# LayerNorm sums from VectorE to ScalarE, wider exponentials and another order of the last products, in an attention and MLP kernel

## The chip, the cores and the metric

The kernel runs on one core of a Trainium2 chip. The metric is the device time of one execution in microseconds (us). In what follows PE is TensorE (matmuls; PEld its weight loads), DVE is VectorE, ACT is ScalarE, POOL is GpSimd and SP is SyncE, which here only issues DMAs.

## The reference

There are 8 batch entries, 8 heads, 576 rows and 64 columns per head. First an attention without a score matrix:

```python
q_s = exp(q - max(q, -1));  q_s /= sum(q_s, -1)          # over the 64 columns
k_s = exp(k - max(k, 2));   k_s /= sum(k_s, 2)           # over the 576 rows
kv  = einsum('bhsd,bhse->bhde', k_s, v)
x   = einsum('bhsd,bhde->bhse', q_s, kv)                  # -> (8, 576, 512)
```

Then, on each row of x (512 columns), a LayerNorm with a gain and a two-layer MLP with a residual:

```python
xn  = (x - mean(x)) / sqrt(var(x) + 1e-6) * g_ln
out = x + relu(xn @ w_ch1) @ w_ch2                        # w_ch1 512x2048, w_ch2 2048x512
```

## The kernel before, in words

**Stages.** The rows are handled as nine chunks c of 512 rows (`T` = 4 tiles of 128). Chunks 0 to 7 are the first 512 rows of the batch entries; chunk 8 (`C9`) collects the 64 rows that each of the eight entries has over. Every chunk goes through the MLP once: a stage. A stage's matmuls are written as a list of steps by `mlp_steps`, and `run` merges a list of side jobs into it: a side job is a pair of a step number and a function, and its instructions are put into every engine's program just ahead of that step. The order is by hand (`tc.manual_schedule`): each engine executes its own instructions in the order in which the program writes them. So "step 34" in what follows is a place in this order, not a time.

**One stage.** For c of 2 (`FAST`) and more, steps 0 to 64 are the first layer, `mm1` (L347): 16 groups of four matmuls of 512 columns into a PSUM tile `ph`, each followed by a relu on ACT (L335) into `hT`. There are six PSUM buffers for these and the second layer's tiles (`mm_ps`), and two for the attention (`att_ps`). Steps 64 to 120 are the second layer, `mm2_fast`: seven products of 16 matmuls of 256 columns each (`prod`, L454; half a step per matmul), in place of eight, after a scheme of Strassen's kind. It needs sums of blocks of `hT` (`sum_h`, L438, DVE), sums of the weights (made once), and sums of the products: ACT copies the accumulating bank `a` at three points (`seed_c` at L548, and `copy_u` at L493 for `s2` and `s3`), and DVE adds these copies to bank `b` (`add_u`, L496; `seed_e` puts one sum into bank `e`). `y_quarter` (L468, DVE) makes a quarter of an output tile: the bank times `rstd` plus `x`. When both halves of a tile are there, POOL stores it.

**Beside it.** In stage c stand, as side jobs, the attention of chunk c + 1 (`attn_fast`) and the preparation of entry c + 2 (`load_batch`, `prep_fast`):

- `load_batch` at step 1 loads q, k, v over SP; a write by DVE into each buffer ahead of it (L818) makes the load wait until the buffer's last reader is done. `qt` has two buffers, `kt` and `vt` one.
- `prep_fast` puts on ACT the exponentials of q (`exp_q`, L175) and of k (`exp_k`, L142), two heads or 512 columns at a time, casts of v (`cast_v`, L150), and the left-over rows of k and v (`prep_kvrem`). `eq_T` transposes the exponentials by a DMA from SP.
- `attn_fast` has the 20 `kv_mm` matmuls, then 4 `po_mm` for each tile t. `x_out` on DVE takes `po` from PSUM: the product with the reciprocal sums (L314), then `stats`: `bn_stats` (L300), `bn_aggr` (L301), and `xn` = (x - mean) * gain (L302). `xn_T` at steps 60 and 101 transposes `xn` by DMA from SP, two tiles at a time; the next stage's `mm1` reads both. `rstd_op` on ACT gives 1/sqrt(var + eps) as an exponential of a logarithm (L328, L329).
- In stage 7 the attention is that of chunk 8, with `attn_side`: 16 `po_mm` of 256 columns at even distances from step 14 to 92, products in four parts per tile (L292), and the same `stats`.

**The last stage** (chunk 8) has no side jobs but `sum_h`. Its products are ordered by `last_products`: the product 4 goes last, into a bank of its own (`d`), with `pre` adding the rest of that quarter beforehand. Tiles 2 and 3 are stored by halves of 256 columns (`store_rest`), 64 rows over SP and 64 over ACT, tiles 0 and 1 whole over POOL.

Of the kernel before, what the change touches and what calls it, by code (L numbers as in the profile page):

```python
# [14 lines left out]
AF = mybir.ActivationFunctionType  # L15
ALU = mybir.AluOpType
# [4 lines left out]
def kernel(  # L21
# [21 lines left out]
    P = 128  # L43
# [90 lines left out]

    eks, eqs, eqTs, xs, xnTs, rstds = {}, {}, {}, {}, {}, {}

    def exp_k(b, j):
        kt = raws[b][0]
        if j == 0:
            eks[b] = att.tile([P, T, H, D], BF16, tag="ek", name="ek")  # L140
        hs = slice(2 * j, 2 * j + 2)
        nc.scalar.activation(  # L142
            eks[b][:, :, hs, :].rearrange("p t h d -> p h t d"), kt[:, hs], AF.Exp
        )
# [23 lines left out]
        )  # L168
        eqTs[c] = att.tile([P, T, NP, P], BF16, tag="eqT", name="eqT")

    def exp_q(b, j):
        if j == 0:
            new_eq(b)
        hs = slice(2 * j, 2 * j + 2)
        nc.scalar.activation(  # L175
            eqs[b][0][:, :, hs, :].rearrange("p t h d -> p h t d"),
            raws[b][2][:, hs], AF.Exp,
        )
# [119 lines left out]
    def stats(c, t, src):  # L298
# [5 lines left out]
            op0=ALU.subtract, op1=ALU.mult,  # L304
        )

    def x_out(c, t):

        x = xs[c][0]
        if c == 1 or (c == 0 and t < 2):  # L310
            stats(c, t, pobox[c, t])
            return
        if c < B:
            nc.vector.tensor_mul(  # L314
                x[:, t].rearrange("p (h d) -> p h d", h=H),
                pobox[c, t].rearrange("p (h d) -> p h d", h=H),
                eqs[c][2][:, t].to_broadcast([P, H, D]),
            )
        stats(c, t, x[:, t])
# [4 lines left out]
    def rstd_op(c):  # L324
        mv = xs[c][3]
        lnv = sml.tile([P, T], FP32, tag="lnv", name="lnv")
        rstds[c] = mlp.tile([P, T], FP32, tag="rstd", name="rstd")
        nc.scalar.activation(lnv, mv[:, :, 1], AF.Ln, bias=eps_ln)  # L328
        nc.scalar.activation(rstds[c], lnv, AF.Exp, scale=-0.5)  # L329

    def relu(i, dst, src, fast):
# [105 lines left out]
        )[i]  # L437
        nc.vector.tensor_tensor(out=dst, in0=x, in1=y, op=op)  # L438

    def prod(n, bank, t, k, first=False, last=False, own=False):  # L440

        at = slice(t * P, t * P + P)
        if n in (1, 2, 4):
            odd, half = ((0, 0), (1, 0), None, (1, 1))[n - 1]
            lhsT = hbox["h"][:, 2 * k + odd, 2 * half + t, :]
        else:
            lhsT = hbox["s"][:, {5: 0, 6: 1, 7: 2, 3: 3}[n], k, at]
        if n in (1, 2):
            rhs = w2_sb[:, 2 * k + n - 1, 0:DH2]
        elif n == 3:  # L450
            rhs = w2_sb[:, 2 * k + 1, DH2:DM]
        else:
            rhs = w2_q[:, {5: 0, 6: 1, 7: 2, 4: 3}[n], k]
        nc.tensor.matmul(hbox[bank][:, t], lhsT, rhs, start=first and (own or t == 0) and k == 0,  # L454
                         stop=k == KH - 1, skip_group_check=True)

    def bank(name):
        hbox[name] = mm_ps.tile([P, 2, DH2], FP32, tag="m", name="b" + name)

    def new_y(c, t):  # L460
        if (c, t) not in ybox:
            ybox[c, t] = outp.tile([P, DM], FP32, tag="ot", name="ot")
            ynum[c, t] = 0

    def y_quarter(c, t, col, src, add=None):
        new_y(c, t)
        cols = slice(DH2 * col, DH2 * col + DH2)
        nc.vector.scalar_tensor_tensor(  # L468
            ybox[c, t][:, cols], in0=src, scalar=rstds[c][:, t : t + 1],
            in1=xs[c][0][:, t, cols] if add is None else add, op0=ALU.mult, op1=ALU.add,  # L470
        )
        ynum[c, t] += 1
        if c == C9:
            if t >= 2:
                store_rest(t, cols)
            elif ynum[c, t] == 2:
                store_rest(t, slice(0, DM))
        elif ynum[c, t] == 2:
            nc.gpsimd.dma_start(  # L479
                out[c, 0:SM, :].rearrange("(p t) n -> p t n", t=T)[:, t], ybox[c, t]  # L480
            )

    def store_rest(t, cols):
        for half, eng in enumerate((nc.sync, nc.scalar) if t >= 2 else (nc.gpsimd, nc.gpsimd)):
            eng.dma_start(
                out[2 * t + half, SM:S, cols], ybox[C9, t][64 * half : 64 * half + 64, cols]
            )

    ybox, ynum = {}, {}

# [4 lines left out]
    def add_u(dst, src):  # L495
        nc.vector.tensor_tensor(out=hbox[dst], in0=hbox["b"], in1=hbox[src], op=ALU.add)  # L496

    def last_products(c, steps, product, seed_c, seed_e):

        def ys(name, col, t0):  # L500
            return [lambda t=t: y_quarter(c, t0 + t, col, hbox[name][:, t]) for t in range(2)]

        def pre(t):
            new_y(c, t)
            nc.vector.scalar_tensor_tensor(
                ybox[c, t][:, 0:DH2], in0=hbox["a"][:, t - 2], scalar=rstds[c][:, t : t + 1],
                in1=xs[c][0][:, t, 0:DH2], op0=ALU.mult, op1=ALU.add,
            )

        def end(t, k):  # L510
            if k == 0:
                bank("d")
            prod(4, "d", t, k, first=True, own=True)
            if k == KH - 1:
                y_quarter(c, 2 + t, 0, hbox["d"][:, t], ybox[c, 2 + t][:, 0:DH2])

        product(1, "a", first=True, at={0: [lambda i=i: sum_h(1, i) for i in range(4)], 15: [seed_c]})
        product(5, "b", first=True)
        product(6, "a", at={15: [lambda: copy_u("s2")]})
        product(2, "c", last=True, at={7: [seed_e]})  # L520
        product(7, "a", at={2: ys("c", 0, 0)[:1], 5: ys("c", 0, 0)[1:], 15: [
            lambda: copy_u("s3"), lambda: pre(2), lambda: pre(3)]})
        product(3, "e", last=True, at={13: [lambda: add_u("b", "s3")] + ys("b", 1, 2)})
        steps += [(0.5, lambda t=t, k=k: end(t, k)) for t in range(2) for k in range(KH)]
        steps.insert(-15, (0, lambda: [fn() for fn in ys("e", 1, 0)]))

    def mm2_fast(c):

        steps = []

        def product(n, name, first=False, last=False, at=None):
            at = at or {}
            for t in range(2):
                for k in range(KH):
                    i = t * KH + k

                    def go(t=t, k=k, i=i):
                        if i == 0 and first:
                            bank(name)
                        prod(n, name, t, k, first, last)  # L540
                        for fn in at.get(i, []):
                            fn()

                    steps.append((0.5, go))

        def seed_c():
            bank("c")
            nc.scalar.copy(hbox["c"], hbox["a"])  # L548

        def seed_e():  # L550
            bank("e")
            add_u("e", "s2")

        if c == C9:
            last_products(c, steps, product, seed_c, seed_e)
            return steps

        def ys(name, col, t0):
            return [lambda t=t: y_quarter(c, t0 + t, col, hbox[name][:, t]) for t in range(2)]

        product(1, "a", first=True, at={
            0: [lambda i=i: sum_h(1, i) for i in range(4)], 15: [seed_c]})
        product(5, "b", first=True)
        product(6, "a", at={15: [lambda: copy_u("s2")]})
        product(2, "c", last=True, at={7: [seed_e]})
        product(7, "a", at={2: ys("c", 0, 0)[:1], 5: ys("c", 0, 0)[1:], 15: [lambda: copy_u("s3")]})
        product(3, "e", last=True, at={13: [lambda: add_u("b", "s3")]})
        product(4, "a", last=True, at={
            1: ys("e", 1, 0)[:1], 4: ys("e", 1, 0)[1:],
            7: ys("b", 1, 2)[:1], 10: ys("b", 1, 2)[1:], 15: ys("a", 0, 2)})  # L570
        return steps
# [78 lines left out]

    def prep_fast(b):

        s = spread([lambda j=j: exp_q(b, j) for j in range(NP)], 40, 62)
        s += [(63, lambda: eq_T(b)), (66, lambda: prep_kvrem(b))]
        s += spread([lambda j=j: exp_k(b, j) for j in range(NP)], 70, 104)
        s += spread([lambda j=j: cast_v(b, j, nc.scalar) for j in range(NP)], 75, 109)
        return s

    def sums_fast(c, t0=0):
# [5 lines left out]
    def attn_fast(c):  # L665
# [5 lines left out]
        s += [(21, lambda: start_x(c))]  # L671
        for t, (p0, p1) in enumerate(((22, 28), (34, 42), (60, 70), (80, 92.5))):
            s += spread([lambda t=t, i=i: po_mm(c, t, i) for i in range(NP)], p0, p1)
            s += [(p1, lambda t=t: x_out(c, t))]
        s += [(60, lambda: xn_T(c, 0, 2)), (101, lambda: xn_T(c, 2, 2)), (105, lambda: rstd_op(c))]
        return s

    def norm_q(b, t):
        eq, zq, rq = eqs[b]
# [144 lines left out]
    with tc.manual_schedule(  # L824
# [43 lines left out]
        for c in range(1, B):  # L868
# [10 lines left out]
            else:  # L879
                if c + 1 < B:  # L880
                    side += attn_fast(c + 1)
                else:
                    side += sums_fast(C9, 2) + attn_side(C9, 0, 0, 14, 92)
                side += [(33 + 3 * i, lambda i=i: sum_h(0, i)) for i in range(4)]
                if c + 2 < B:
                    side += [(1, lambda b=c + 2: load_batch(b))]
# [41 lines left out]
```

## Time and profile before

| | |
|---|---|
| Median of 7 runs | 296.86 us (295.41 to 297.45) |
| Profiled execution, its own time | 296.77 us |
| Span of the profile | 295.0 us |
| Mean granted clock of PE | 0.989 |
| Instructions | 5124 |
| Busy: PE, DVE, ACT, POOL | 275.9, 216.0, 158.3, 28.9 us |
| Bytes moved by DMA | 49.04 MB |

The span runs from the first to the last instruction on the core; 1.77 us of the execution's time lie outside it. Busy time of an engine is the time in which at least one of its instructions was under way. Stages 3, 4, 5 and 6 start at 118.8, 147.0, 175.1 and 203.15 us, stage 7 at 231.1, stage 8 at 260.6, and the last matmul starts at about 286.5 us. In rows of a timeline the columns are start, duration, engine, line, operation, output and input, shapes, count, and in square brackets the idle time ahead of it and what ended it.

### The profile page before, as it was taken

To read this page: it belongs to the slowest core of one execution; us is meant where nothing else is said; L and a number is where in the kernel's file an instruction comes from. 1 tells how busy PE (TensorE), PEld (TensorE's weight loads), DVE (VectorE), ACT (ScalarE), POOL (GpSimd) and SP (SyncE) were. 2 spreads that over 40 slices of the span, in tenths; PEclk is the share of its full clock that TensorE was granted. 3 is DMA by queue.
4 is the path that set the end of the run, shared out by engine and by line. 5 is a ranking of instruction groups with operands and counts; after the bars stand their busy time and mean duration, and the time that the engine had idled before them with its cause. 6 is when DMAs were issued, how large, how long until landed. Compare 5 with 4: busy or idle time off the path is not lost.

```text
span 295.0 us, 5124 instructions
## 1 busy us (share of the span) xinstructions
PE 275.9 (94%) x2012; PEld 179.5 (61%) x2017; DVE 216.0 (73%) x451; ACT 158.3 (54%) x293; POOL 28.9 (10%) x61
## 2 busy tenths in 40 slices
PE   7869998999998999999999999999999999899980
PEld 2648845545544478548854875587568647754870
DVE  4656398596997679787978897799678879933370
ACT  3536693478344694488458825973663363236310
POOL 3500030110011000200110020002000200020002
PEclk9979999999999999999999999999999999999998
DMA  7999979966999991799289839936513501040004
GB/s 188 211 209 260 249 163 211 304 233 172 345 132 234 343 169 36 238 341 134 55 282 306 111 108 309 264 72 170 152 36 73 178 1 38 19 163 0 0 16 129
DMA packets 74171, 49.04 MB, mean 166 GB/s; under 512 B 42273, under 2 KB 71969, under 8 KB 74146
## 3 DMA queue, kind: packets, MB, share of 16 engines
q1 hardware_dynamic: 66050, 34.74, 49.7%
q0 software_dynamic: 7776, 13.70, 19.1%
q8 instruction: 16, 0.26, 0.4%
q10 hardware_dynamic: 320, 0.26, 0.3%
q14 instruction: 9, 0.07, 0.1%
HBM read 36.70 MB, written 9.44 MB: 156 GB/s over the span
## 4 chain that ended last, share of the span: by engine, by line
PE 74%; DVE 10%; DMA 8%; ACT 3%; issue 1%; SPq 1%; POOL 1%; POOLq 0%; ACTq 0%
PE ph L347 33%; PE ba L454 14%; PE pc L396 4%; PE be L454 4%; PE bb L454 4%; PE bc L454 4%; DMA eqT<-eq 3%; PE pc L407 3%; DMA qt<-in_q_dram 3%; PE ph L362 2%; DMA kt<-in_k_dram 2%; PE po L276 2%; PE pkv L244 2%; DVE x L292 2%; DVE hs L438 2%; DVE st L300 2%
## 5 line engine op out<-in xcount | busy, mean ns | idle before, releaser
L347 PE MATMUL ph<-xnT,w_sb 128*128 128x512 bf16 x528 | 126.4, 379 | 0.0
L335 ACT ACTIVATE hT<-ph 128x512 bf16<-128x512 f32 x129 | 76.3, 596 | 60.2 <-PE ph L347 60.1
L347 PEld LDWEIGHTS <-w_sb 128*128 128x128 bf16 x528 | 49.4, 98 | 53.8 <-DMA xnT<-xn 0.3
L454 PEld LDWEIGHTS <-hs 128*128 128x128 bf16 x448 | 43.2, 98 | 6.1 <-issue 1.0
L454 PEld LDWEIGHTS <-hT 128*128 128x128 bf16 x336 | 32.2, 98 | 4.5
L438 DVE TENSOR_TENSOR hs<-hT 128x1024 bf16<-128x1024 bf16 x28 | 19.2, 687 | 19.3 <-ACT hT L335 19.3
L479 POOL DMA_DIRECT2D out_dram<-ot x24 | 12.9, 540 | 159.0 <-DVE ot L468 159.0
L454 PE MATMUL ba<-w_q,hs 128*128 128x256 bf16 x224 | 27.6, 273 | 0.0
L276 PE MATMUL po<-kv_sb,eqT 128*128 128x128 bf16 x128 | 24.3, 219 | 2.9 <-DMA eqT<-eq 1.4
L302 DVE SCALAR_TENSOR_TENSOR xn<-x,mv,g_bc 128x512 bf16<-128x512 bf16 x30 | 22.6, 752 | 1.1
L244 PE MATMUL pkv<-vm,ek 128*128 128x129 bf16 x112 | 22.6, 220 | 0.4 <-DVE vm L152 0.3
L314 DVE TENSOR_TENSOR x<-po,rq 128x512 bf16<-128x512 f32 x26 | 17.8, 683 | 6.4 <-PE po L276 6.2
L493 ACT COPY s<-ba 128x512 f32<-128x512 f32 x14 | 8.2, 586 | 25.6 <-PE ba L454 25.6
L300 DVE BATCH_NORM_STATS2 st<-x 128x6 f32<-128x512 bf16 x30 | 20.8, 694 | 1.0
L276 PEld LDWEIGHTS <-eqT 128*128 128x128 bf16 x128 | 11.7, 97 | 11.1 <-issue 1.9
L142 ACT ACTIVATE ek<-kt 128x512 bf16<-128x512 f32 x28 | 16.8, 625 | 0.1
L175 ACT ACTIVATE eq<-qt 128x512 bf16<-128x512 f32 x24 | 14.6, 626 | 3.6 <-DMA qt<-in_q_dram 3.6
L407 PE MATMUL pc<-w_sb,hT 128*128 128x512 bf16 x61 | 15.6, 379 | 0.2
L396 PE MATMUL pc<-w_sb,hT 128*128 128x512 bf16 x62 | 14.6, 379 | 0.1
L454 PE MATMUL be<-w_sb,hs 128*128 128x256 bf16 x112 | 13.4, 273 | 0.8 <-DVE be L496 0.8
L454 PE MATMUL ba<-w_sb,hT 128*128 128x256 bf16 x112 | 14.0, 273 | 0.0
L662 DVE TENSOR_REDUCE zq<-eq 128x8 f32<-128x512 bf16 x22 | 13.9, 691 | 0.0
(102 smaller groups left out, 339.8 us busy)
## 6 DMA issues: line engine op xcount, KB each, us to landing
out_dram<-ot POOLq DMA_DIRECT2D x32, 256.0 KB, 3.3
qt<-in_q_dram SPq DMA_DIRECT2D x7, 1024.0 KB, 7.2
vt<-in_v_dram SPq DMA_DIRECT2D x7, 1024.0 KB, 12.5
kt<-in_k_dram SPq DMA_DIRECT2D x6, 1024.0 KB, 9.7
w_sb<-in_moe_w_ch_dram POOLq DMA_DIRECT2D x8, 512.0 KB, 10.8
kt<-in_k_dram SPq DMA_DIRECT2D x4, 288.0 KB, 5.9
qt<-in_q_dram SPq DMA_DIRECT2D x2, 512.0 KB, 6.6
kt<-in_k_dram SPq DMA_DIRECT2D x2, 512.0 KB, 9.2
```

Of the source, the lines that this page charges most:

```text
L142: nc.scalar.activation(eks[b][:, :, hs, :].rearrange("p t h d -> p h t d"), kt[:, hs], AF.Exp)
L244: nc.tensor.matmul(pkv[:, j % 2, 0:w], lhsT, rhs, start=(t == 0), stop=(t == last))
L276: nc.tensor.matmul(pobox["p"][:, i * P : i * P + P], eqTs[c][:, t, i, :], kv_sb[:, c, i, :], start=True, stop=True,)
L300: nc.vector.bn_stats(st[:, t], src)
L302: nc.vector.scalar_tensor_tensor(xn[:, t], in0=src, scalar=mv[:, t, 0:1], in1=g_bc, op0=ALU.subtract, op1=ALU.mult,)
L314: nc.vector.tensor_mul(x[:, t].rearrange("p (h d) -> p h d", h=H), pobox[c, t].rearrange("p (h d) -> p h d", h=H), eqs[c][2][:, t].to_broa ...
L335: nc.scalar.activation(dst, src, AF.Relu)
L347: nc.tensor.matmul(hbox["ph"], w1_sb[:, ko, m * P : (m + 1) * P], xnTs[c][:, :, ko, :], start=(ko == 0), stop=(ko == KO1 - 1),)
L396: nc.tensor.matmul(hbox["pc"], hbox["h"][:, ko, t, :], w2_sb[:, ko, :], start=(ko == 0), stop=(ko == KO2 - 1),)
L407: nc.tensor.matmul(hbox["pc", t], hbox["h"][:, ko, t, :], w2_sb[:, ko, :], start=(ko == 0), stop=(ko == KO2 - 1),)
L438: nc.vector.tensor_tensor(out=dst, in0=x, in1=y, op=op)
L454: nc.tensor.matmul(hbox[bank][:, t], lhsT, rhs, start=first and (own or t == 0) and k == 0, stop=k == KH - 1, skip_group_check=True)
```

## The change

Statistics. `bn_stats` and `bn_aggr` go for chunks 3 to 8. For chunks 3 to 7, `x_fast` lets the DVE product also give the row sum (an accumulator output), scales it to the negative mean, and makes `xn` by adding it; a Square on ACT with the negative mean as its bias and an accumulator output gives the sum of squared differences (`square_sum`), and the division by 512 goes into the logarithm of `rstd_op`. For chunk 8, whose product is in four parts, ACT gives both sums: a Copy with an accumulator and a Square (`x_rest`), and DVE adds the mean later (`xn_out`). Chunk 8's attention gets step numbers of its own (`attn_rest`).

Exponentials. In `prep_fast` (entries 4 to 7) those of q and k take four heads at a time, 1024 columns, and all its jobs have new steps: `exp_q` 34 and 73 (before: four from 40 to 56), `eq_T` 77 (63), `prep_kvrem` 82 (66), `exp_k` 90 and 106 (four from 70 to 95), `cast_v` 76, 79, 95, 99 (75 to 100).

Last products. Product 4 goes back into bank `a`, product 2 is split into its two tiles with product 7 between them, and product 3 goes last, a tile at a time, into two banks `e0` and `e1` that DVE fills beforehand. All tiles are stored whole, 64 rows over SP and 64 over POOL.

```diff
-    def exp_k(b, j):
+    def exp_k(b, j, hn=2):
...
-        hs = slice(2 * j, 2 * j + 2)
+        hs = slice(2 * j, 2 * j + hn)
...
+    def square_sum(c, t):
+        x, _, _, mv = xs[c]
+        nc.scalar.activation(
+            junk, x[:, t], AF.Square, bias=mv[:, t, 0:1], accum_out=mv[:, t, 1:2]
+        )
+
+    def xn_out(c, t):
+        x, _, xn, mv = xs[c]
+        nc.vector.scalar_tensor_tensor(
+            xn[:, t], in0=x[:, t], scalar=mv[:, t, 0:1], in1=g_bc, op0=ALU.add, op1=ALU.mult
+        )
+
+    def x_fast(c, t):
+        x, st, _, mv = xs[c]
+        nc.vector.scalar_tensor_tensor(
+            x[:, t].rearrange("p (h d) -> p h d", h=H),
+            in0=pobox[c, t].rearrange("p (h d) -> p h d", h=H), scalar=1.0,
+            in1=eqs[c][2][:, t].to_broadcast([P, H, D]), op0=ALU.mult, op1=ALU.mult,
+            accum_out=st[:, t, 0:1],
+        )
+        nc.vector.tensor_scalar_mul(out=mv[:, t, 0:1], in0=st[:, t, 0:1], scalar1=-1.0 / DM)
+        xn_out(c, t)
+
+    def x_rest(t):
+        x, _, _, mv = xs[C9]
+        nc.scalar.activation(
+            junk, x[:, t], AF.Copy, scale=-1.0 / DM, accum_out=mv[:, t, 0:1]
+        )
+        square_sum(C9, t)
...
-        nc.scalar.activation(lnv, mv[:, :, 1], AF.Ln, bias=eps_ln)
+        nc.scalar.activation(
+            lnv, mv[:, :, 1], AF.Ln, bias=eps_ln, scale=1.0 / DM if c > FAST else 1.0
+        )
...
         if c == C9:
-            if t >= 2:
-                store_rest(t, cols)
-            elif ynum[c, t] == 2:
-                store_rest(t, slice(0, DM))
+            if ynum[c, t] == 2:
+                store_rest(t, (nc.sync, nc.gpsimd))
...
+        def seed(t):
+            bank("e%d" % t)
+            nc.vector.tensor_tensor(
+                out=hbox["e%d" % t][:, t], in0=hbox["b"][:, t], in1=hbox["s2"][:, t], op=ALU.add
+            )
...
-        product(2, "c", last=True, at={7: [seed_e]})
-        product(7, "a", at={2: ys("c", 0, 0)[:1], 5: ys("c", 0, 0)[1:], 15: [
-            lambda: copy_u("s3"), lambda: pre(2), lambda: pre(3)]})
-        product(3, "e", last=True, at={13: [lambda: add_u("b", "s3")] + ys("b", 1, 2)})
-        steps += [(0.5, lambda t=t, k=k: end(t, k)) for t in range(2) for k in range(KH)]
-        steps.insert(-15, (0, lambda: [fn() for fn in ys("e", 1, 0)]))
+        product(2, "c", ts=(0,))
+        product(7, "a", at={2: [lambda: seed(0), lambda: seed(1)], 15: [lambda: copy_u("s3")]})
+        product(2, "c", ts=(1,), at={10: [lambda: add_u("b", "s3")], 15: ys("c", 0, 0)})
+        product(4, "a", at={10: ys("b", 1, 2), 15: ys("a", 0, 2)})
+        product(3, "e0", ts=(0,), at={7: ys("e0", 1, 0)[:1]})
+        product(3, "e1", ts=(1,), at={15: ys("e1", 1, 0)[1:]})
...
-        s = spread([lambda j=j: exp_q(b, j) for j in range(NP)], 40, 62)
-        s += [(63, lambda: eq_T(b)), (66, lambda: prep_kvrem(b))]
-        s += spread([lambda j=j: exp_k(b, j) for j in range(NP)], 70, 104)
-        s += spread([lambda j=j: cast_v(b, j, nc.scalar) for j in range(NP)], 75, 109)
+        s = [(34, lambda: exp_q(b, 0, 4)), (73, lambda: exp_q(b, 2, 4)), (77, lambda: eq_T(b))]
+        s += [(82, lambda: prep_kvrem(b))]
+        s += [(90, lambda: exp_k(b, 0, 4)), (106, lambda: exp_k(b, 2, 4))]
+        s += [(p, lambda j=j: cast_v(b, j, nc.scalar)) for j, p in enumerate((76, 79, 95, 99))]
...
-            s += [(p1, lambda t=t: x_out(c, t))]
+            s += [(p1, lambda t=t: x_fast(c, t)), ((40, 52, 89, 105)[t], lambda t=t: square_sum(c, t))]
...
+    def attn_rest():
+        s = sums_fast(C9, 2) + [(12, lambda: start_x(C9))]
+        for t, (p0, p1, p2, p3) in enumerate(
+            ((14, 28, 31, 42), (29, 46, 56, 62), (50, 68, 76, 83), (70, 86, 92, 100))
+        ):
+            s += spread([lambda t=t, i=i: po_mm(C9, t, i) for i in range(NP)], p0, p1)
+            s += [(p2, lambda t=t: x_rest(t)), (p3, lambda t=t: xn_out(C9, t))]
+        return s + [(66, lambda: xn_T(C9, 0, 2)), (102, lambda: xn_T(C9, 2, 2)), (107, lambda: rstd_op(C9))]
...
-                    side += sums_fast(C9, 2) + attn_side(C9, 0, 0, 14, 92)
+                    side += attn_rest()
```

More of the change, by code (lines that the diff above doesn't have):

```diff
@@ L169, in new_eq, with exp_q @@
         eqTs[c] = att.tile([P, T, NP, P], BF16, tag="eqT", name="eqT")
-    def exp_q(b, j):
+    def exp_q(b, j, hn=2):
         if j == 0:
             new_eq(b)
-        hs = slice(2 * j, 2 * j + 2)
+        hs = slice(2 * j, 2 * j + hn)
         nc.scalar.activation(
@@ L438, in sum_h, with prod @@
         nc.vector.tensor_tensor(out=dst, in0=x, in1=y, op=op)
-    def prod(n, bank, t, k, first=False, last=False, own=False):
+    def prod(n, bank, t, k, first=False, last=False):
         at = slice(t * P, t * P + P)
@@ L453, in prod @@
             rhs = w2_q[:, {5: 0, 6: 1, 7: 2, 4: 3}[n], k]
-        nc.tensor.matmul(hbox[bank][:, t], lhsT, rhs, start=first and (own or t == 0) and k == 0,
+        nc.tensor.matmul(hbox[bank][:, t], lhsT, rhs, start=first and t == 0 and k == 0,
                          stop=k == KH - 1, skip_group_check=True)
@@ L458, in bank, with y_quarter @@
         hbox[name] = mm_ps.tile([P, 2, DH2], FP32, tag="m", name="b" + name)
-    def new_y(c, t):
+    def y_quarter(c, t, col, src):
         if (c, t) not in ybox:
@@ L463, in new_y @@
             ynum[c, t] = 0
-    def y_quarter(c, t, col, src, add=None):
-        new_y(c, t)
         cols = slice(DH2 * col, DH2 * col + DH2)
@@ L469, in y_quarter @@
             ybox[c, t][:, cols], in0=src, scalar=rstds[c][:, t : t + 1],
-            in1=xs[c][0][:, t, cols] if add is None else add, op0=ALU.mult, op1=ALU.add,
+            in1=xs[c][0][:, t, cols], op0=ALU.mult, op1=ALU.add,
         )
@@ L481, in y_quarter, with store_rest @@
             )
[L483 to L487, printed above, removed]
+    def store_rest(t, engines):
+        for half, eng in enumerate(engines):
+            eng.dma_start(out[2 * t + half, SM:S, :], ybox[C9, t][64 * half : 64 * half + 64])
     ybox, ynum = {}, {}
@@ L496, in add_u, with last_products @@
         nc.vector.tensor_tensor(out=hbox[dst], in0=hbox["b"], in1=hbox[src], op=ALU.add)
-    def last_products(c, steps, product, seed_c, seed_e):
+    def last_products(c, steps, product, seed_c):
         def ys(name, col, t0):
             return [lambda t=t: y_quarter(c, t0 + t, col, hbox[name][:, t]) for t in range(2)]
[L503 to L507, printed above, removed]
-            )
[L510 to L515, printed above, removed]
+        def seed(t):
+            bank("e%d" % t)
+            nc.vector.tensor_tensor(
+                out=hbox["e%d" % t][:, t], in0=hbox["b"][:, t], in1=hbox["s2"][:, t], op=ALU.add
+            )
         product(1, "a", first=True, at={0: [lambda i=i: sum_h(1, i) for i in range(4)], 15: [seed_c]})
@@ L519, in last_products, with product @@
         product(6, "a", at={15: [lambda: copy_u("s2")]})
-        product(2, "c", last=True, at={7: [seed_e]})
-        product(7, "a", at={2: ys("c", 0, 0)[:1], 5: ys("c", 0, 0)[1:], 15: [
-            lambda: copy_u("s3"), lambda: pre(2), lambda: pre(3)]})
-        product(3, "e", last=True, at={13: [lambda: add_u("b", "s3")] + ys("b", 1, 2)})
-        steps += [(0.5, lambda t=t, k=k: end(t, k)) for t in range(2) for k in range(KH)]
-        steps.insert(-15, (0, lambda: [fn() for fn in ys("e", 1, 0)]))
+        product(2, "c", ts=(0,))
[4 more added lines that the diff above has]
+        product(3, "e1", ts=(1,), at={15: ys("e1", 1, 0)[1:]})
     def mm2_fast(c):
         steps = []
-        def product(n, name, first=False, last=False, at=None):
+        def product(n, name, first=False, last=False, at=None, ts=range(2)):
             at = at or {}
-            for t in range(2):
+            for t in ts:
                 for k in range(KH):
@@ L554, in mm2_fast @@
         if c == C9:
-            last_products(c, steps, product, seed_c, seed_e)
+            last_products(c, steps, product, seed_c)
             return steps
```

## The prediction

> **What bounds the kernel now.** I read the page's busy totals first, then a table by stage, then the timelines of the stages that are not full. The core has one stage per batch entry, c = 0 to 7, and a stage 8 for the left-over rows (C9 in the code). The table of windows (columns: span, then busy time of PE, PEld, DVE, ACT, POOL) reads:
>
> ```profile
> PE 275.9 (94%) x2012; PEld 179.5 (61%) x2017; DVE 216.0 (73%) x451; ACT 158.3 (54%) x293; POOL 28.9 (10%) x61
> ...
> 118.80:147.00 28.20, 28.20 (x214) 19.20 (x212) 23.43 (x49) 18.06 (x34) 2.13 (x5) 1.00 0.80 196
> 147.00:175.10 28.10, 28.10 (x214) 19.14 (x212) 23.24 (x49) 17.91 (x34) 2.18 (x5) 1.00 0.80 198
> 231.20:260.70 29.50, 28.11 (x194) 18.68 (x192) 25.27 (x51) 11.70 (x21) 2.94 (x6) 1.00 0.19 54
> 286.80:295.00 8.20, 0.00 (x0) 0.00 (x0) 1.09 (x3) 0.00 (x0) 2.12 (x4) 0.82 0.48 128
> ```
>
> Stages 3 to 6 have no hole on PE, though DVE is at 23 of 28 us and ACT at 18: work taken off DVE or put on ACT there is worth nothing, as long as PE stays fed. Stage 7 has holes. Its need: 64 matmuls of 512 columns take 13.81 us (260.73 to 274.54 in the chain, stage 8, which has nothing between them), 112 of 256 columns take 7 x 1.75 = 12.25, and 16 `po` at 0.109 take 1.75; together 27.81 against 29.51 (231.05 to 260.56, first matmul to first matmul). So 1.70 us are lost. The timeline names the places:
>
> ```profile
> 251.15 0.28 PE L283 MATMUL po<-kv_sb,eqT 128*128 128x256 bf16 x1 [0.55 <-DVE x L292]
> 257.07 1.91 PE L454 MATMUL be<-w_sb,hs 128*128 128x256 bf16 x16 [0.84 <-DVE be L496]
> ...
> 254.59 0.69 DVE L300 BATCH_NORM_STATS2 st<-x 128x6 f32<-128x512 bf16 x1
> 255.32 0.18 DVE L301 BATCH_NORM_AGGREGATE mv<-st 128x2 f32<-128x6 f32 x1
> 255.54 0.75 DVE L302 SCALAR_TENSOR_TENSOR xn<-x,mv,g_bc 128x512 bf16<-128x512 bf16 x1
> 256.32 0.70 DVE L496 TENSOR_TENSOR be<-bb,s 128x512 f32<-128x512 f32 x1
> ```
>
> Start to start, the holes are 251.15 - (249.88 + 5 x 0.109) = 0.72 and 257.07 - (254.32 + 16 x 0.109) = 1.00: 1.72, the whole loss. Both wait for DVE, which has worked almost without a gap since 237.95; the adding of `be` stands behind the last tile's statistics.
>
> The third part is the tail, in the timeline and at line 485:
>
> ```profile
> 285.45 0.88 DVE L468 SCALAR_TENSOR_TENSOR ot<-bb,rstd,x 128x256 f32<-128x256 f32 x2
> 286.24 0.86 DVE L468 SCALAR_TENSOR_TENSOR ot<-be,rstd,x 128x256 f32<-128x256 f32 x2
> 287.01 2.12 POOL L485 DMA_DIRECT2D out_dram<-ot  x4 [24.39 <-DVE ot L468]
> 287.02 0.86 DVE L468 SCALAR_TENSOR_TENSOR ot<-bd,rstd,ot 128x256 f32<-128x256 f32 x2
> ```
>
> PE's last product ends at 286.6, DVE's last output at 287.88, and POOL is issuing its fourth store until 289.13. The chain ends in that store; some 3.5 us of flight and the end of the program follow. Stage 2 also loses 1.37 us, waiting for the DMA of `eqT`; the change doesn't touch what comes before it.
>
> **The change, part by part.**
>
> Statistics of stage 7 (for C9): DVE loses the statistics (238.84 to 239.57: 0.73) and their aggregation (0.21), four times: 3.76 us. ACT gains a Copy and a Square, each with an accumulator, per tile. The trace has no accumulator. Below: a plain 128x512 one, 0.52 start to start (three in 1.67). Above: 0.62 with 0.09 for a per-partition bias (`lnv` 298 ns against `rstd` 205) and one more short instruction, 0.20: 0.92. I take 0.62 and 0.70, nearest to the rows of 512: 5.3 us on an ACT that idles 17.8 us of this stage. At the first hole two tiles' statistics are gone (1.88 against 0.72), at the second four (3.76 against 1.00), so both should close: -1.6, keeping 0.1 for new friction. What is late next: `be` needs the copy of `s` on ACT (252.78 + 0.58) and 0.70 on DVE, 254.1, and is wanted at 256.07, so 2 us are left. The last `xn` now stands at step 100, behind two outputs: it ends some 0.9 us past that step, the transpose lands 3.0 after its issue (the row of this stage), and 40 matmuls or 4.38 us remain: 0.4 spare. ACT's pair at step 56 is followed by only two relus before the stage's second half; I find the last relu 0.5 us late, against 0.7 that `sum_h` and product 5 have to spare. These two thin margins are my 0.1.
>
> Statistics of stages 3 to 7 (stages 2 to 6 compute them): per tile DVE goes from 0.73 + 0.73 + 0.21 + 0.67 (start to start, from 154.23) to a product with accumulator, a tiny scaling and `xn`. The product lies between 0.68 (the row of L314) and 0.95 (the 0.75 of L302 and a short instruction); I take 0.85, with 0.2 and 0.67: 0.6 less per tile, 2.4 per stage. ACT gains four Squares, 2.8 us. Both are hidden by PE's full stages: 0. If that cover went, it is ACT's 2.8 us against its 10 us of idle time. The queue behind matters more: relus stand behind the Squares at steps 40 and 52, and PE has six banks, so it would wait only after several of them; by step 64 three relus' gaps (0.3 to 0.4 each) have taken in 0.7.
>
> A rule speaks against this: the Trainium skill, ScalarE: Activation LUTs, section Rules for kernel authors, sends additions and multiplications to VectorE, which is faster per element. By it, 1.32 us of ACT replace 0.94 of DVE per tile of stage 7, and the four tiles would lose 1.5 us. The trace decides otherwise: the engine that ends last at both holes is DVE, while ACT waits for PE (7.0 us at L493 alone in this stage). I take the trace, -1.6.
>
> Wider exponentials: eight of 128x512 become four of 128x1024. From 625 ns at 512 and 832 at 768 columns (L212) I estimate 1.04 us, 0.95 start to start, against 2 x 0.52: 0.4 less per stage, hidden: 0. The longer one holds a relu up by 0.5 more. The first now comes at step 34, when q must be there: q lands at 127.56 (120.36 + 7.2), ACT reaches that place at 127.7 after the eighth relu, and in the next stages at 155.6 against 155.9 and 183.3 against 184.0. Just enough; a microsecond late would be borne by the banks. `eq_T` moves on SP from step 63 to 77, past no other transfer: issued near 166.2 and landing 4.3 later at 170.5, ahead of `xn_T` at 171.1. k's exponentials end near step 117, the memset that frees `kt` comes 2 us later, so the loads don't move. The remainder's preparation, moved to step 82, no longer waits for its DMA (1.2 us on ACT, hidden): 0. Scaling inside Ln is free.
>
> Tail (clock of the run before). Product 6 ends at 279.62. Product 2 is split, so product 7 comes 0.88 later and needs the copy, done at 280.41: no wait, within 0.05; the same for product 4 (copy done 283.04, wanted 283.12). PE's count of matmuls is unchanged, its end stays at 286.6. DVE: sum for `b` 283.06, outputs of `c` 283.7, of `b` 284.5, of `a` 285.35, `e0` 286.15, `e1` after PE's end at 286.85, done 287.3 instead of 287.88. POOL issues at 0.53 each: first at 285.8, the fourth at 287.4 to 287.93, against 289.13. SP issues the other halves at 0.55. The stores are the same megabyte, now in eight. The end follows POOL: -1.2; I take -1.1.
>
> Against it stands the skill's DMA: Bandwidth & Descriptors, section Issuing engine by pattern: Sync and Scalar are generally faster issuers than GpSimd (Specifications gives 0.6 against 1 us to the first byte). By it, the stores moved from ACT to POOL cost 0.4 and the tail gains 0.7. Here POOL's stores took 535 ns to issue and 3.5 us to land, ACT's 662 ns and 4.3 us, so I keep -1.1.
>
> Sum: -1.6 - 1.1 = -2.7 on a profiled execution of 296.77 (span 295.0, 1.77 around it), which is 0.09 under the median of 296.86: 294.1.
>
> **The rivals.** (1) Stage 7's holes close but reopen elsewhere, behind a late relu or the late transpose (0.4 spare), or the tail's stores collide; only one of the two gains comes: 295.2 to 296. For it: thin margins. Against: DVE's slack grows by 3.8 us. (2) Slower: ACT's accumulators cost more than 0.92. At the end of the first half of each stage 2 to 6, relus then end over 0.7 us late and product 5 waits for `sum_h`. It decides from about 1.2 us per Square; at 1.6 each of five stages would lose some 0.8, +4.0, against -1.1 for the tail and nothing from stage 7: 299.8. For it: PE has no other cover there. Against: ACT's plain rows are 0.6. A Square outside the loaded table set is the extreme of it: one load took 1283 ns, and 24 Squares with two loads each, 62 us of ACT, would end far above 320. (3) The change doesn't do what it says: only the product order matters because PE bounds everything: -1.1 or less, 295.7 and up.
>
> **How the numbers follow.** Both gains 0.64 (own range 293.3 to 294.9), one gain 0.19 (half of it beyond 0.3%, or 0.89 us, about what a measurement of this kernel can tell from no change), slower by ACT 0.13, slower by a collision at the end 0.04. Faster 0.72, same 0.12, slower 0.16. The range takes in the case of one gain and a tail better by 0.8: 293.0 to 296.6.
>
> **What would show it.** Right: no hole on PE in stage 7, which spans 27.8 to 28.1; stages 3 to 6 at 28.1 as now; no L300 rows after stage 2; Square near 0.7; the last DVE output 0.6 and POOL's last store 1.2 nearer to PE's end. Wrong: table loads on ACT, PE waits released by ACT `hT` or DVE `hs`, an `xnT` DMA that PE waits for at a stage's start, or a store issued by DVE later than PE's end + 0.7.

## The result, and the profile after

The changed kernel takes 293.01 us in the median (12 runs), against 296.59 us (31 runs) for the kernel before: ratio 0.9884, 95% interval 0.9862 to 0.9906, or 3.4 us (2.8 to 4.1). Measured again on another occasion (22 runs against 75) it was 0.9898 (0.9871 to 0.9926), or 3.0 us. The forecast was 2.7 us. The profiled execution of the changed kernel took 291.83 us, its span is 290.1.

The same two views as before. The page's busy line and the table of windows (span, then busy time of PE, PEld, DVE, ACT, POOL) for a full stage, stage 7 and the time after the last matmul:

```profile
PE 273.6 (94%) x2012; PEld 178.5 (62%) x2017; DVE 198.4 (68%) x442; ACT 176.5 (61%) x333; POOL 28.9 (10%) x61
...
144.60:172.67 28.07, 28.07 (x215) 19.23 (x213) 20.57 (x50) 20.51 (x38) 2.15 (x5) 1.00 0.80 197
228.76:256.76 28.00, 28.00 (x195) 18.59 (x193) 21.26 (x42) 16.88 (x37) 2.21 (x5) 1.00 0.20 57
283.00:290.10 7.10, 0.00 (x0) 0.00 (x0) 0.48 (x1) 0.00 (x0) 1.31 (x3) 0.80 0.50 148
```

DVE gave up 17.6 us in all and ACT took on 18.2. Stage 4 (the first of the three rows) still takes 28.07 us, with DVE at 20.6 and ACT at 20.5 in place of 23.2 and 17.9: that exchange bought nothing there. Stage 7 has no hole left: PE is busy 28.00 of 28.00, which is 0.19 above the 27.81 that the prediction added up; two matmuls near the stage's middle start about 0.1 us late each.

Its timelines (PE first, then DVE, then ACT), at the place where the second hole was:

```profile
251.52 1.91 PE L488 MATMUL ba<-w_q,hs 128*128 128x256 bf16 x16
253.27 1.91 PE L488 MATMUL be<-w_sb,hs 128*128 128x256 bf16 x16
256.76 13.98 PE L381 MATMUL ph<-xnT,w_sb 128*128 128x512 bf16 x64
...
250.92 0.70 DVE L523 TENSOR_TENSOR be<-bb,s 128x512 f32<-128x512 f32 x1
252.51 0.74 DVE L315 SCALAR_TENSOR_TENSOR xn<-x,mv,g_bc 128x512 bf16<-128x512 bf16 x1
...
250.46 0.64 ACT L334 ACTIVATE junk<-x 128x512 bf16<-128x512 bf16 x1
250.99 0.19 ACT L334 ACTIVATION_READ_ACCUMULATOR junk<-x 128x1 f32 x1
251.21 0.72 ACT L309 ACTIVATE junk<-x,mv 128x512 bf16<-128x512 bf16 x1
251.84 0.19 ACT L309 ACTIVATION_READ_ACCUMULATOR junk<-x,mv 128x1 f32 x1
```

`be` is filled at 251.62 and wanted at 253.27: 1.65 us to spare where 1.00 was missing. The last `xn` ends at 253.25, its transpose is issued at once and lands at 256.32, some 3.0 later, and the next stage starts on time at 256.76: 0.4 to spare. An accumulator on ACT is read by an instruction of its own, 0.19 us.

The tail, in the timeline (the first row is two outputs, the second POOL's four stores):

```profile
281.43 0.87 DVE L499 SCALAR_TENSOR_TENSOR ot<-ba,rstd,x 128x256 f32<-128x256 f32 x2
282.20 2.11 POOL L514 DMA_DIRECT2D out_dram<-ot  x4 [23.39 <-DVE ot L499]
283.00 0.48 DVE L499 SCALAR_TENSOR_TENSOR ot<-be,rstd,x 128x256 f32<-128x256 f32 x1 [0.32 <-PE be L488]
```

DVE's last output now waits for PE and ends 0.5 us after PE's modelled end (282.96); before it was 1.1 us (287.89 after 286.77). POOL's last store is issued 1.35 us after PE's end (284.31) in place of 2.35 (289.12).

Where the time went can be read stage by stage, since every stage starts with a matmul that the PE timeline shows. Each row is worked out from the starts of the first matmuls in one profile (in that of before 118.64, 146.85, 174.91, 202.98, 231.05 and 260.56 us; the starts given ahead of the prediction for stages 3 to 6 are up to 0.2 us later). "Tail" is from the start of stage 8 to the end of the span, which the page gives to 0.1 us. The rows under the second are the experiments.

| Kernel | stage 3 | stages 4 to 6, each | stage 7 | tail |
|---|---|---|---|---|
| before | 28.21 | 28.07 | 29.51 | 34.44 |
| changed | 28.07 | 28.07 | 28.00 | 33.34 |
| changed, second time | 28.07 | 28.07 | 28.01 | 33.47 |
| before + tail | 28.30 | 28.07 | 29.52 | 33.31 |
| before + stage 7 | 28.64 | 28.07 | 28.01 | 34.40 |
| before + hidden parts | 28.07 | 28.07 | 29.52 | 34.40 |
| changed, stores SP + ACT | 28.07 | 28.06 | 28.01 | 31.81 |
| before, stores SP + ACT | 28.07 | 28.07 | 29.53 | 32.49 |

The figures repeat well: where stage 7 is the same program, its time agrees within 0.02 us. So stage 7 gave 1.51 us and the tail 1.10: 2.6 of the 2.7 forecast. Stage 3 gave 0.14 more.

The two spans differ by 4.9 us, more than these parts, because stage 3 starts at 118.64 in the one and at 116.49 in the other, and 1.95 of these 2.15 us are there when stage 2 starts (89.02 and 87.07), up to where the programs are the same. That is scatter and no part of the gain: over the 13 profiles of this case stage 2 starts anywhere from 87.07 to 89.58. The granted clock doesn't explain it. In the stretch from 15 to 30 us it was 0.89 in five profiles, that of before among them, and 1.00 in the other eight; stage 2 starts from 88.27 to 89.42 in the five and from 87.07 to 89.58 in the eight.

### The profile page after: what moved, and what is told of

It is laid out like the page before. It is cut to its first block, busy times and chain, and to the rows that moved or that the text cites. A ratio compares the mean times of both kernels' runs of the same rounds, so it can differ in the third digit from the quotient of the medians.

```text
span 290.1 us, 5164 instructions
## 1 busy us (share of the span) xinstructions
PE 273.6 (94%) x2012; PEld 178.5 (62%) x2017; DVE 198.4 (68%) x442; ACT 176.5 (61%) x333; POOL 28.9 (10%) x61
## 4 chain that ended last, share of the span: by engine, by line
issue 64%; PE 13%; DVE 6%; POOL 5%; DMA 5%; ACT 3%; SPq 1%; POOLq 0%; ACTq 0%; DVEq 0%
PE ph L381 5%; POOL out_dram L508 4%; PE pc L441 3%; DMA qt<-in_q_dram 3%; PE ph L396 2%; DMA kt<-in_k_dram 2%; DVE st L300 2%; DVE xn L302 1%; DVE x L346 1%; PE ptr L715 1%; ACT ek L142 1%; ACT hT L369 1%; POOL out_dram L418 1%; PE pkv L244 1%; ACT eqT L717 1%
## 5 line engine op out<-in xcount | busy, mean ns | idle before, releaser
L369 ACT ACTIVATE hT<-ph 128x512 bf16<-128x512 f32 x129 | 75.2, 595 | 46.6 <-PE ph L381 46.4
L315 DVE SCALAR_TENSOR_TENSOR xn<-x,mv,g_bc 128x512 bf16<-128x512 bf16 x24 | 18.0, 752 | 0.8
L322 DVE SCALAR_TENSOR_TENSOR x<-po,rq 128x512 bf16<-128x512 f32 x20 | 13.7, 686 | 6.1 <-PE po L276 6.1
L309 ACT ACTIVATE junk<-x,mv 128x512 bf16<-128x512 bf16 x24 | 17.3, 720 | 0.2
L175 ACT ACTIVATE eq<-qt 128x512 bf16<-128x512 f32 (+1 forms) x16 | 13.1, 840 | 3.4 <-DMA qt<-in_q_dram 3.2
L142 ACT ACTIVATE ek<-kt 128x512 bf16<-128x512 f32 (+1 forms) x20 | 15.1, 790 | 0.0
L488 PE MATMUL bc<-w_sb,hT 128*128 128x256 bf16 x112 | 13.8, 273 | 0.0
```

Of the source, the lines that this page charges most:

```text
L142: nc.scalar.activation(eks[b][:, :, hs, :].rearrange("p t h d -> p h t d"), kt[:, hs], AF.Exp)
L309: nc.scalar.activation(junk, x[:, t], AF.Square, bias=mv[:, t, 0:1], accum_out=mv[:, t, 1:2])
L315: nc.vector.scalar_tensor_tensor(xn[:, t], in0=x[:, t], scalar=mv[:, t, 0:1], in1=g_bc, op0=ALU.add, op1=ALU.mult)
L369: nc.scalar.activation(dst, src, AF.Relu)
```

## The experiments

**The three parts alone, and all of them again.** The edits are the hunks of the diff, sorted: (a) the last products and stores; (b) `x_rest`, `attn_rest` and the scale of the logarithm for chunk 8; (c) `x_fast`, `square_sum`, the new steps and widths of `prep_fast`; (d) the changed kernel.

> The kernel before with the new order of the last products and the whole-tile stores over SP and POOL, and nothing else of the change. My theory: the tail is worth about 1.1 us by itself (ratio 0.996), the last DVE output follows the last matmul's start by about 0.6 us instead of 1.3 and POOL's fourth store is issued 1.2 us earlier; stage 7 keeps its holes of 0.7 and 1.0 us. Rival A (the landing of the stores, not their issue, sets the end): under 0.4 us. Rival B (the part of the gain beyond my 2.7 us comes from the tail, ACT's DMA queue no longer being used): 1.8 us or more.

> The kernel before with stage 7 alone changed: chunk 8's statistics on ACT and the new step numbers. Theory: both holes close, stage 7 takes 28.0 us instead of 29.5, ratio 0.994 to 0.995 (1.5 to 1.8 us). Rival (the holes only move, to a late relu or the transpose): under 0.5 us.

> The kernel before with the two parts that I priced at nothing: statistics of chunks 3 to 7 shared by DVE and ACT, and the wide exponentials with their new steps. Theory: stages 3 to 6 stay at 28.07 us each, ratio 1.000 within 0.002. Rival (the 0.8 us by which the whole change did better than forecast lie here, for example in stage 2 or 3): 0.997. Rival (relus late): above 1.003.

> The changed kernel as it is, on the same chip as its parts. Theory: the parts add up, 1.1 + 1.7 + 0 = 2.8 us, ratio 0.9905, and what the first measurement showed beyond it (3.4 us) is its scatter. Rival (the parts help one another, or a part that I priced at nothing counts): the ratio stays at 0.988, below the product of the three parts' ratios.

Measured: (a) 0.9977 (0.9948 to 1.0007), (b) 0.9955 (0.9929 to 0.9981), (c) 1.0000 (0.9974 to 1.0027), (d) 0.9898 (0.9871 to 0.9926). The product of the parts is 0.9932, just above (d)'s interval, but each part has an interval of about 0.003 to either side; by time alone it isn't settled whether some 1.0 us (0.0034 of 296.9) come from their acting together. Nor is (a) by itself clear of no change, by time. The table is sharper: the tail is 33.31 with (a) alone, stage 7 is 28.01 with (b) alone, the values of the whole change. Nothing there needs two parts at once. Part (c) gains in stage 3 only, and the profile of (b), where it is lacking, shows what (PE timeline, then ACT):

```profile
137.98 0.93 PE L488 MATMUL ba<-w_q,hs 128*128 128x256 bf16 x7 [0.41 <-ACT bc L582]
...
136.16 0.63 ACT L157 ACTIVATE ekr<-ktr 64x512 bf16<-64x512 f32 x1 [1.62 <-DMA ktr<-in_k_dram]
137.35 0.58 ACT L582 COPY bc<-ba 128x512 f32<-128x512 f32 x1
```

ACT stands still for a DMA at the old step 66, and behind it in its queue is the copy of bank `a` that PE's product 6 waits for. The four profiles that had the old step there differ by when the DMA landed: ACT waited 0.88, 1.19, 1.29 and 1.62 us for it, and stage 3 took 0, 0.14, 0.23 and 0.57 us more than 28.07. In every profile with step 82 it took 28.07, but for those with repeated Squares below.

**Which half of stage 7's edit closes the holes?** First the new steps without the move to ACT (with the scale in the logarithm of chunk 8 taken out again, not shown), then the move with the even steps of `po`, close to the old ones. The second keeps the new steps of `xn` and of its transposes (`xn_out`, the last number of each group). These two kernels and those with repeated Squares below ran once each, so only stages of their profiles are compared:

```diff
-            s += [(p2, lambda t=t: x_rest(t)), (p3, lambda t=t: xn_out(C9, t))]
+            s += [(p2, lambda t=t: x_out(C9, t))]
...
```

```diff
-            ((14, 28, 31, 42), (29, 46, 56, 62), (50, 68, 76, 83), (70, 86, 92, 100))
+            ((14, 33.5, 33.5, 42), (33.5, 53, 56, 62), (53, 72.5, 76, 83), (72.5, 92, 92, 100))
```

> The changed kernel with chunk 8's statistics left on DVE (bn_stats and bn_aggr, as before) but at the new step numbers. Tells the two halves of stage 7's gain apart. If moving the statistics off DVE closes the holes (my theory): stage 7 takes about 29.5 us again. If the new step numbers do it: 28.0.

> The changed kernel with chunk 8's statistics on ACT but its po matmuls at even distances again, near the old steps (14 to 92). Complement of the run with the statistics left on DVE. If either half of the change closes the holes by itself: stage 7 takes 28.0 to 28.3. If it is the new steps that do most of it: 28.6 or more, with a PE wait on DVE x.

Stage 7 took 28.30 and 28.28 us. Each half alone is worth 1.2 us, both together 1.5. What is left over (PE timeline, then DVE, for the second ACT too; the first kernel and then the second):

```profile
257.96 6.22 PE L381 MATMUL ph<-xnT,w_sb 128*128 128x512 bf16 x28 [0.35 <-DMA xnT<-xn]
...
252.42 0.70 DVE L523 TENSOR_TENSOR be<-bb,s 128x512 f32<-128x512 f32 x1
253.15 0.69 DVE L300 BATCH_NORM_STATS2 st<-x 128x6 f32<-128x512 bf16 x1
```

```profile
250.35 0.28 PE L283 MATMUL po<-kv_sb,eqT 128*128 128x256 bf16 x1 [0.23 <-DVE x L292]
255.27 1.91 PE L488 MATMUL be<-w_sb,hs 128*128 128x256 bf16 x16
...
246.80 0.69 DVE L472 TENSOR_TENSOR hs<-hT 128x1024 bf16<-128x1024 bf16 x1 [0.87 <-ACT hT L369]
249.43 1.75 DVE L292 TENSOR_TENSOR x<-po,rq 64x256 bf16<-64x256 f32 x4
252.85 0.70 DVE L523 TENSOR_TENSOR be<-bb,s 128x512 f32<-128x512 f32 x1
254.52 0.74 DVE L315 SCALAR_TENSOR_TENSOR xn<-x,mv,g_bc 128x512 bf16<-128x512 bf16 x1
...
253.45 0.18 ACT L334 ACTIVATION_READ_ACCUMULATOR junk<-x 128x1 f32 x1
```

With DVE's statistics at the new steps the filling of `be` stands ahead of the last tile's statistics and comes in time; only the transpose of the last `xn` is late. With ACT's statistics at the even steps only the first of the two old holes is left, 0.23 us of idle time where it was 0.55: DVE, freed of the statistics, waits 0.87 us for a relu, and four sums `hs` stand between that and the `x` that PE needs. It is the new `po` steps that close this hole. The second hole is closed, and not only because `be` stands ahead of the last `xn` in this kernel too: ACT's sum for that `xn` is there at 253.63, so with `xn` in front `be` would be ready at about 255.1 (an estimate from these rows), still ahead of 255.27.

**How much can ACT bear?** The Square of chunks 3 to 7 two times and, with `range(3)`, three times (the line's first part is left out):

```diff
-            s += [..., ((40, 52, 89, 105)[t], lambda t=t: square_sum(c, t))]
+            s += [..., ((40, 52, 89, 105)[t], lambda t=t: [square_sum(c, t) for _ in range(2)])]
```

> Each Square with its accumulator twice in chunks 3 to 7: ACT has some 1.5 us per tile there instead of 0.75 (the result is the same). My second rival said that stages 2 to 6 would stall from about 1.2 us per Square. If that threshold is right, stages 3 to 6 grow from 28.07 by 0.1 to 0.5 us each. If ACT's slack is larger: they stay at 28.07.

> Each Square three times, some 2.2 us per tile. By the rival's price stages 2 to 6 lose some 1.5 us each, with PE waits on ACT hT, DVE hs or the copies of bank a. If the slack is larger than I thought: under 0.3 us each, and nothing in stages where the wait falls behind the first layer.

Twice: stages 3 to 6 take 28.43, 28.58, 28.25 and 28.22 us. Three times: 32.76, 30.75, 33.39 and 29.92. So the slack ends before the second Square is done, as the rival said. The third Squares are some 3.4 us of ACT per stage, four of 0.85 us. They add 4.3 and 5.1 us to stages 3 and 5, but 2.2 and 1.7 to stages 4 and 6. The timeline of stage 3 shows the difference:

```profile
138.09 1.79 PE L488 MATMUL ba<-w_sb,hT 128*128 128x256 bf16 x9 [2.33 <-ACT hT L369]
139.67 2.99 PE L488 MATMUL bb<-w_q,hs 128*128 128x256 bf16 x16
```

PE waits 2.33 us for a relu, in the middle of product 1 and not in product 5 as the rival had it, and then its 16 matmuls take 2.99 us where they took 1.91 in every stage above. The granted clock was 0.95 in this stage and in stage 5, and 1.00 in stage 4, which waited 2.12 us and stayed at full clock. By windows (the granted clock is the third number from the end):

```profile
135.04:138.45 3.41, 1.08 (x12) 0.78 (x10) 0.00 (x0) 3.35 (x9) 0.00 (x0) 1.00 1.22 86
138.45:141.86 3.41, 3.41 (x19) 2.43 (x17) 3.24 (x7) 2.01 (x4) 0.00 (x0) 0.50 0.01 1
```

For 3.41 us PE runs at half clock, which costs up to 1.7 us on top of the wait.

**Whose queue stores last?** The changed kernel with ACT's queue in POOL's place, and then the kernel before, old order of products, with the same:

```diff
-                store_rest(t, (nc.sync, nc.gpsimd))
+                store_rest(t, (nc.sync, nc.scalar))
```

```diff
-        for half, eng in enumerate((nc.sync, nc.scalar) if t >= 2 else (nc.gpsimd, nc.gpsimd)):
+        for half, eng in enumerate((nc.sync, nc.scalar)):
```

> The changed kernel with the last stores' second halves on ACT's DMA queue in place of POOL's. If issue on POOL (534 ns, 3.2 to 3.6 us to land) is the better, as I priced it against the rule of the skill: from the last stage's first matmul to the end of the span 33.4 us becomes 33.6 to 33.9. If the rule holds (Sync and Scalar are the faster issuers): 33.0.

> The kernel before, with the stores of the last stage's tiles 0 and 1 over SP and ACT in place of POOL; the order of the last products stays. If POOL's stores alone set the end of the kernel before: the tail (from the last stage's first matmul) falls from 34.4 to about 32.6 us, more than the 1.1 us that the new order with POOL brought. If the order of products is what counts: 34.0 or more.

The first is 0.9865 (0.983 to 0.990) of before, with a tail of 31.81 us: 1.5 less than the changed kernel's. (By time alone the two can't be told apart, their intervals overlap.) The second is 0.9925 (0.9891 to 0.9958), tail 32.49. I had the sign wrong in the first. The second shows that taking POOL's queue out of the old tail is worth 1.95 us, more than the new order with its whole-tile stores, which is worth 1.1 with POOL's queue (34.44 to 33.31) and 0.7 without (32.49 to 31.81). What the queue costs is in the end of the program, in the rows of its last line (engine, kind, count, shortest/median/longest in ns, first and last start). The changed kernel from 280 us on, then the one with ACT's queue from 280 us on and, last row, from 250 to 280:

```profile
L952 SPq EVENT_SEMAPHORE  x11: 17/28/2849, 284.4 to 290.0; - x11
L952 POOLq DRAIN  x3: 51/102/5518, 283.8 to 289.8; - x3
```

```profile
L952 SPq EVENT_SEMAPHORE  x11: 17/28/28, 285.6 to 289.6; - x11
L952 POOLq DRAIN  x2: 51/76/102, 289.1 to 289.4; - x2
...
L952 POOLq DRAIN  x1: 4802/4802/4802, 259.4 to 259.4; - x1
```

After its last store POOL drains its queue for 5.5 us, from 283.8 to 289.3, and only then does the program end, though SP's longest wait ends at 287.4. In the kernel before, that drain took 5.8 us. Its length is mostly the flight of the stores; what counts is its end. In all ten profiles with POOL stores at the end it ends 1.92 to 1.93 us after POOL's last store has landed (here 287.35), and the span ends 0.79 us after that. With ACT's queue POOL drains just so after its last stores of stage 7, for 4.8 us from 259.4 on, where nothing waits for it. The last store then lands as long after PE's end as before, 4.6 us in both kernels (287.57 and 288.67), but the span ends 1.0 us after it in place of 2.5. That difference is the 1.5 us. It wasn't tried whether a store of another size shortens the drain.

**Both further gains in one kernel.** Stores over SP and ACT (the edit above, not shown again), and in stage 2 the first tile's `po_mm` at steps 29 to 34 in place of 22 to 28, after the transpose of `eqT` has landed:

```diff
-        for t, (p0, p1) in enumerate(((22, 28), (34, 42), (60, 70), (80, 92.5))):
+        for t, (p0, p1) in enumerate(((29, 34) if c == 3 else (22, 28), (35, 42) if c == 3 else (34, 42), (60, 70), (80, 92.5))):
...
-            s += [(p1, lambda t=t: x_fast(c, t)), ((40, 52, 89, 105)[t], lambda t=t: square_sum(c, t))]
+            s += [(p1, lambda t=t: x_fast(c, t)), ((43 if c == 3 else 40, 52, 89, 105)[t], lambda t=t: square_sum(c, t))]
```

> The changed kernel with the last stores over SP and ACT, and with the first tile of chunk 3's attention later in stage 2 (steps 29 to 34 in place of 22 to 28), where PE waits 1.2 us for the DMA of eqT. If both are what they seem: stage 2 loses its hole, the tail takes 31.8 us, 2.7 us less than the changed kernel, ratio to before about 0.980. If the eqT hole only moves on (the transpose lands later still, or the statistics become late): 1.5 us less, 0.985.

It takes 291.06 us (6 runs), 0.9828 of before (0.9778 to 0.9878); that is below the changed kernel's 0.9884 and 0.9898, but the intervals still overlap a little. Stage 2, from its first matmul to stage 3's, is now without a hole:

```profile
88.86:116.93 28.07, 28.07 (x213) 19.23 (x213) 20.25 (x48) 20.24 (x38) 1.84 (x4) 1.00 0.94 199
```

It took 29.62 us before and 29.42 in the changed kernel. The tail is 31.70. So by stages it is 1.35 and 1.6 us shorter than the changed kernel.

## Why the prediction was right

- **Stage 7: right in size, but its reason is only one of two.** -1.6 was forecast, -1.51 came. I put it all down to the statistics leaving DVE, which by itself gives 1.2 us. The new steps give as much with the statistics left on DVE, and I gave them no share: the working counted how much earlier DVE's work would come, but not that the order alone takes the filling of `be` out from behind the statistics. At the first hole the working was wrong: 1.88 us less of statistics did not close 0.72, because DVE then waits for a relu; the earlier `po` steps close it. So it is in part luck that both holes went. The margin that I named for the last transpose was real: 0.4 forecast, 0.4 measured, and with the statistics on DVE the transpose was late.
- **Stages 3 to 6: the nothing was right** for the statistics and the exponentials. The terms measured, with what I had assumed in brackets: x with its accumulator 0.73 from start to start (0.85), the scaling 0.19 (0.2), Square 0.70 to 0.72, and 0.85 ahead of the logarithm (0.70), Copy 0.75 (0.62), the wide exponentials 1.04 to 1.06 long (1.04). One nothing was wrong: `prep_kvrem`'s wait of 1.2 us on ACT, which I had as hidden, held up a copy behind it and cost PE 0.14 us in that profile, up to 0.57 in others. The wait was in the trace; I didn't ask who was queued behind it.
- **The rule about ScalarE** (the Trainium skill, ScalarE: Activation LUTs, Rules for kernel authors) was rightly set aside: ACT's pair took 1.46 us from start to start against 0.94 on DVE, as the rule has it, but with the new steps in both kernels the move made stage 7 0.3 us shorter (28.30 to 28.00), not longer.
- **The tail: right in size, -1.1 forecast and 1.10 measured, and right that the end follows POOL's last store, but the weighing of the queues was wrong.** POOL's last store came 1.0 us nearer to PE's end (1.2 forecast). I compared issue and landing of POOL's and ACT's stores and set aside the rule of the Trainium skill, DMA: Bandwidth & Descriptors, Issuing engine by pattern, which favours Sync and Scalar. Moving the stores to SP and ACT gains 1.5 us more. The rule's sign holds here, but not because stores land sooner (the last lands 4.6 us after PE's end either way): POOL's drain ends only 1.93 us after its last landing, which no issue or landing time shows. The old trace had this drain (5.8 us).
- **The slower rival** set ACT's slack at about 1.2 us per Square. At twice (some 1.55 us) stages lost 0.15 to 0.5, so the threshold was about right; 0.7 us was under it. The place was another: PE waited for a relu in product 1. There was one table load of 1283 ns in the whole program, as before, so the Square needed none of its own.
- **The rest, 0.7 us between the first ratio and the forecast,** is 0.14 from stage 3 and otherwise not explained: the forecast lies just outside the first interval (2.8 to 4.1 us) and inside the second (2.2 to 3.8). The median of 293.01 us is at the very edge of the range that I gave (293.0 to 296.6); that of the second occasion, 294.26, lies well inside. The start of stage 2, which differs by up to 2.5 us from execution to execution, is wider than what is missing.

## What to carry to other kernels

Where one engine is full, cost a move by who is queued behind what on every other engine, not by busy time: 2.7 us less of DVE per stage was worth nothing in the full stages, and in stage 7, where DVE ended last, a mere change of order with the work left on DVE gave 1.2 of the 1.5 us, as much as the move did by itself. Before giving a queue the last stores, look at what the program's end waits for: a queue whose stores land as fast may still take 1.5 us longer to close. And a stall that waits for a DMA may be hidden in one profile and cost time in the next.

## What the runs showed of the hardware that I had not expected

- POOL's drain after its last store ends 1.92 to 1.93 us after that store has landed, in all ten profiles where this is the end of the program; it is 5.4 to 5.8 us long there. Where POOL's last stores are those of stage 7, it is 4.8 us long and costs nothing.
- An accumulator output is read by an instruction of its own: 0.19 us on ACT, 0.08 us on DVE.
- Whether a wait lowers PE's clock depends on where it falls. In the 13 traces the granted clock changes only in whole multiples of 3.41 us: between two changes lie, for example, 13.65, 61.44 or 133.12 us (4, 18 and 39 times 3.413), and every drop ahead of the last matmul lasts 3.41 us, at half clock. There are seven of them. In the 3.41 us ahead of each, PE was busy for 0.93 to 1.55 us; cut into the same stretches, no other stretch ahead of the last matmul has less than 1.57 us, and none was followed by a drop. So it is not the length of one wait that counts but how much PE stood still within such a stretch: in one profile a wait of 1.93 us came with a drop, shorter waits standing beside it in the stretch; in another a wait of 2.35 us, shared by two stretches with 2.06 and 1.91 us of work, came without one. PE's ends are modelled, so a limit between 1.55 and 1.57 us is only as exact as the model.
